# One-core attention, mixture-of-experts and bilinear kernel: head 0 prepared first, similarities turned by transposes, 256- and 512-token chunks mixed in the second stage

## The chip, the cores and the metric

The kernel runs on one core of a Trainium2 chip. The time is device microseconds (us) of one launch; three runs of the kernel before gave 778.71, 779.07 and 779.94 us, median 779.07. Beside them one execution was profiled.

The engines, by the profile's names: PE is TensorE (matrix products; PEld is its load of the stationary operand), DVE is VectorE, ACT is ScalarE, POOL is GpSimd, SP is SyncE, which here only issues transfers. SBUF is the on-chip memory, PSUM the eight banks that PE writes its sums to. Each engine works through its own list of instructions in order.

## The reference

```python
# 1. attention: B=2, H=8, S=768, D=64, 16 centroids a head
q_assign = argmax(einsum('bhsd,hcd->bhsc', q_n, c_n))   # k_assign likewise
mask     = q_assign[:, :, :, None] == k_assign[:, :, None, :]
attn     = softmax(where(mask, scale * q @ k.T, -1e9))
x        = (attn @ v), heads side by side               # 1536 tokens x 512
# 2. mixture of experts: 8 experts, each token to the one with the largest logit
h = relu(x[mask] @ w1[e]);  out[mask] = gate[mask] * (h @ w2[e])   # F = 1024
# 3. bilinear layer: d_ff = 1536
out = ((x @ w_a) * (x @ w_b)) @ w_out
```
Centroids, queries and keys are divided by their norms before the similarity; for a query's or key's own argmax its own norm does not matter, a centroid's does.

## The kernel before

**Attention.** The 16 pairs of (batch, two heads) are 8 steps of `pp`; each has 12 units `s` (two heads, six tiles of 128 queries). A unit is: `scores` (two products of 512 and two of 256 columns, L550 and L551), `rowmax` (a DVE maximum over 768 keys, L559), `expo` (ACT, L564), `etrans` (six 128x128 transposes, L579, copied out by ACT L583 and DVE L585). Once in six units `pv_gen` multiplies by V (L606). The mask is 16 extra rows of K3 and Q3 that `prep_gen` makes for the next `pp` while the units of this one run; it is a generator, and the loop over `s` takes one or two of its steps per unit (`UNITS`, L802). The steps of `prep_gen`: transposes of split rows of K and Q into K2 and Q2 (L425, through three PSUM banks tagged `rot`); copies of K2, Q2 into K3, Q3 by DMA (L429, L430); similarities to the centroids `sm` (L441), copied to `sim`; `st` (L450), which turns six 128x128 tiles of `sim` by a product with `bothr`, a matrix that adds a centroid's rounded and rest part and multiplies by its reciprocal norm; then in `first_gen` (L455) maximum, comparison, index, maximum, comparison on DVE give the one-hot `oh`; `t2` (L495, L518) transposes it into K3 and Q3.

**The start.** For `pp` 0 there is nothing to hide behind: splitting (`split_rows`, L375), both heads' transposes, both heads' `sm` and `st`, then head 0's one-hot, then `scores(0)`. `setup_centroids` (L301) gives its DVE operations one by one between. `keep_warm` (L258) multiplies ones into an unused tile. `load_qk(1)` uses the buffers of `load_qk(0)` (L219, one buffer each).

**Experts.** The weights stream in through four `raw` buffers and are split in two parts. The change does not touch this.

**Bilinear layer.** The five chunks in `CHUNKS` (L33) are 256, 256, 256, 512 and 256 tokens. The list `order` (L1358) goes through the first three together, four columns of `w_a`, `w_b` (128 wide) for a chunk at a time, 36 steps; then the 512-token chunk, 12 steps, and the last one, 12 steps. A step I is `bil1(I)` (24 products, L1119 within `mm3`, then ACT L1311, DVE L1312, ACT L1313, DVE L1317) and `bil2` of an earlier step (L1352; three products of 512 columns per 128 tokens). `bil1` of a 256-token chunk fills half-banks of `et0` or `et1` in turn; of a 512-token chunk two banks, `et0`, `et1` and `pp`, `pv` in turn. Beside that a step narrows one piece of the 64-bit weights (`narrow_a` to `narrow_d`: ACT, three DVE, ACT, DVE), and `load_raw` then asks for a further piece on SP's queue. `X2` and `X2S` (L34, L35) say at which step a chunk's tokens are loaded (`load_x2`) and split on ACT and DVE (`split_x2`).

Of the kernel before, what the change touches and what calls it, by code (L numbers as in the profile page):

```python
# [22 lines left out]
P = 128  # L23
# [12 lines left out]
I0 = 0  # L36
PACE = (1,)
YW = 1
CG0 = 2
# [3 lines left out]
FL1 = 2  # L43
# [4 lines left out]
def kernel(  # L48
# [186 lines left out]
    load_v(0)  # L235
    emb_sb = att.tile([NE, DM], F32, tag="emb", name="emb_sb", bufs=1)
    nc.sync.dma_start(out=emb_sb, in_=expert_emb)
    tau_sb = left.tile([P, 1], F32, name="tau_sb")
    nc.sync.dma_start(out=tau_sb, in_=tau.rearrange("(o n) -> o n", o=1).to_broadcast([P, 1]))
# [8 lines left out]
    both = att.tile([P, 4 * C], F32, name="both", bufs=1)  # L248
# [4 lines left out]
    nc.vector.tensor_reduce(out=mbi, in_=ident5[:, :, 1, :], axis=AX.XY, op=ALU.add)  # L253
    nc.vector.tensor_scalar(out=msc, in0=mbi, scalar1=FAR, scalar2=1.0, op0=ALU.mult, op1=ALU.max)
    nc.vector.tensor_scalar(out=mbi, in0=mbi, scalar1=-FAR, scalar2=None, op0=ALU.mult)
    nc.vector.tensor_add(both.rearrange("p (s c) -> p s c", s=4), ident5[:, :, 0, :], ident5[:, :, 1, :])
# [78 lines left out]
    nc.gpsimd.memset(cbuf.bitcast(F32), 0.0)  # L335
    nc.gpsimd.iota(iota_c, pattern=[[0, 1], [-1, C]], base=C, channel_multiplier=0, allow_small_or_imprecise_dtypes=True)
    identb = att.tile([P, P], BF16, name="identb", bufs=1)
    nc.gpsimd.tensor_copy(identb, ident)

    def setup_rest():  # L340
# [14 lines left out]
        yield  # L355
        nc.vector.reciprocal(rtau, tau_sb)
# [18 lines left out]
    def split_rows(pp):  # L375
# [6 lines left out]
        hss = (slice(0, 1), slice(1, 2)) if pp == 0 else (slice(0, 2),)  # L382
        for hs in hss:
            nc.scalar.copy(c[:, hs, :, :D], kk[:, hs])
            nc.scalar.activation(a[:, hs, :, D:], qq[:, hs], AF.Copy, scale=scale)
        for hs in hss:
            yield
            if pp == 0:
                nc.vector.tensor_sub(c[:, hs, :, D:], kk[:, hs], c[:, hs, :, :D])
                nc.vector.scalar_tensor_tensor(out=a[:, hs, :, :D], in0=qq[:, hs], scalar=scale, in1=a[:, hs, :, D:], op0=ALU.mult, op1=ALU.subtract)  # L390
            else:
                nc.gpsimd.tensor_sub(c[:, :, :, D:], kk, c[:, :, :, :D])
# [5 lines left out]
    def prep_gen(pp):  # L398
# [13 lines left out]
        def evac(dst, src):  # L412
            n[0] += 1
            if n[0] < 7 or n[0] % 2 if pp == 0 else second[0]:
# [5 lines left out]
        for u in range(3):  # L420
            for dst, src in ((K2, c), (Q2, a)):
                pt = bank(F32R, f"t1_{pp}_{u}")
                for j in range(4):
                    h, i = divmod(4 * u + j, NT)
                    nc.tensor.transpose(pt[:, j * P:(j + 1) * P], src[:, h, i, :], identr)  # L425
                evac(dst[:, u * 512:(u + 1) * 512], pt)
                yield

        nc.sync.dma_start(out=K3[:D].bitcast(F32), in_=K2[:D].bitcast(F32))  # L429
        nc.sync.dma_start(out=Q3[:D].bitcast(F32), in_=Q2[D:].bitcast(F32))  # L430

        groups = ((0,), (1,)) if pp == 0 else ((0, 1),)
        sts = []
        for hs in groups:
            slots = [2 * h + isk for h in hs for isk in range(2)]
            sim = att.tile([P, S], F32, tag="sim", name=f"sim_{pp}", bufs=1)
            for lo, w in ((0, 512), (512, 256)):
                pt = bank(F32, f"sm_{pp}_{lo}")
                for sl in slots:
                    h, isk = divmod(sl, 2)  # L440
                    nc.tensor.matmul(pt[:, :w], cbuf[:, 2 * hp + h, 96 - 32 * sl:224 - 32 * sl],  # L441
                                     (Q2, K2)[isk][:, h * S + lo:h * S + lo + w], start=(sl == slots[0]), stop=(sl == slots[-1]))
                evac(sim[:, lo:lo + w], pt[:, :w])
                yield
            yield
            if pp == 0:
                keep_warm(wps[:, :512], FL1)
            st_ = bank(F32, f"st_{pp}")[:, :NT * 64].rearrange("p (t s c) -> p t s c", s=4, c=C)
            for j in range(NT):
                nc.tensor.matmul(st_[:, j], sim[:, j * P:(j + 1) * P], bothr[:, hp, :], start=True, stop=True)  # L450
            n[0] += 1
            sts.append(st_[:, :, slots[0]:slots[-1] + 1, :])
            yield
# [24 lines left out]
        for hs, st_ in zip(groups, sts):  # L478
            ohs = []
            firsts.append((hs, 2 * len(hs), ohs, first_gen(hs, st_, ohs)))  # L480
        for hs, ns, ohs, fg in firsts:
# [5 lines left out]
            if pp == 0:  # L487
                h = hs[0]
                order = [(1, t) for t in range(NT)] + [(0, t) for t in range(NT)]
                for u in range(0, len(order), 4):  # L490
                    if h == 0:
                        keep_warm(wps[:, :512], FL2)
# [17 lines left out]
                    if h == 0:  # L510
                        next(firsts[1][3])
# [16 lines left out]
            if pp == 0 and h == 0:  # L528
                yield
        yield  # L530
# [229 lines left out]
    next(cg)  # L760
    next(cg)
    sg = split_rows(0)
    next(sg)
    next(sg)
    for _ in range(CG0):
        next(cg)
    drain(sg)
    pg = prep_gen(0)
    for i in range(2):
        keep_warm(wps[:, :512], 5)  # L770
        next(pg)
    for i in range(4):
        next(pg)
        for _ in range(3):
            next(cg, None)
    for _ in range(2):
        next(pg)
    drain(cg)
    rest = setup_rest()
    next(rest)  # L780
# [480 lines left out]
    HD = DC // 2  # L1261

    def load_x2(ck):

        at, wd = CHUNKS[ck]
        if ck == 2:
            x = [big.tile([P, DC, CAP], F32R, tag="xe", name=f"x2{n}_{ck}", bufs=2) for n in "hl"]
            x = [[x[m][:, HD * u:HD * u + HD] for u in range(2)] for m in range(2)]
        elif wd == CAP:
            x = new_x(f"b{ck}")  # L1270
            x = [[x[:, m, HD * u:HD * u + HD] for u in range(2)] for m in range(2)]
        else:
            x = [[rawp.tile([P, HD, wd], F32R, tag="raw", name=f"x2_{ck}{m}{u}") for u in range(2)] for m in range(2)]
        for u in range(2):
            nc.sync.dma_start(out=x[1][u].bitcast(F32), in_=ys_v[:, HD * u:HD * u + HD, at:at + wd])
        xT_t["b", ck] = x

    def split_x2(ck, u):

        hi, lo = (x[u] for x in xT_t["b", ck])  # L1280
# [171 lines left out]
```

## Time and profile before

| | us |
|---|---|
| median of three runs | 779.07 |
| the profiled execution | 778.49 |
| its span (first to last instruction) | 776.4 |
| PE busy in the span | 754.8 |
| DVE, ACT, POOL busy | 462.6, 378.4, 106.1 |

The attention fills the span up to about 293 us, the experts up to about 465, the bilinear layer the rest. PE counts as busy from a product's start to a modelled end, and such ends overlap the next start; so what a group of products costs PE is read from the start of one group to the start of the next, not from its duration. The clock that PE was granted stands at 1.00 in all stretches but the last (0.98).

### The profile page before, as it was taken

The numbers are of one execution on the slowest core, as the hardware profiler recorded it, in microseconds if no ns is written. First come the engines' busy times: TensorE is split into PE (matmuls) and PEld (weight loads), VectorE is DVE, ScalarE is ACT, GpSimd is POOL, SyncE is SP. The second block draws the span as 40 slices with busy tenths as digits, with TensorE's granted clock in tenths as the row PEclk, the third lists the DMA queues.
The fourth block names the chain that finished last, engine by engine and source line by source line (L and its number), as shares of the span: only waits on it lengthen the run. The fifth ranks groups of instructions, "written<-read, shape, count | busy, mean of one in ns | idle before, by whom it ended". The sixth has DMA issues, their size and how long they took to land.

```text
span 776.4 us, 13347 instructions
## 1 busy us (share of the span) xinstructions
PE 754.8 (97%) x5097; PEld 648.5 (84%) x5097; DVE 462.6 (60%) x929; ACT 378.4 (49%) x794; POOL 106.1 (14%) x143
## 2 busy tenths in 40 slices
PE   8899999999999988999999999999999999999996
PEld 5667777777777668999999999999999988888995
DVE  6776665787767776378876898877743221121211
ACT  5656766667675665266654555544423211111211
POOL 6203212051300041000000004420001110000201
PEclk9999999999999999999999999999999999999999
DMA  7228133152221026789879866773401000000100
GB/s 187 60 80 270 45 94 87 59 182 96 60 52 32 28 96 225 271 299 296 276 243 275 280 218 186 154 139 113 136 1 55 28 28 1 0 1 1 55 1 27
DMA packets 48519, 91.91 MB, mean 118 GB/s; under 512 B 6328, under 2 KB 21304, under 8 KB 48448
## 3 DMA queue, kind: packets, MB, share of 16 engines
q1 hardware_dynamic: 44240, 81.01, 35.8%
q0 software_dynamic: 2304, 6.31, 2.1%
q10 hardware_dynamic: 1904, 3.67, 1.3%
q8 instruction: 41, 0.67, 0.3%
q14 instruction: 30, 0.25, 0.1%
HBM read 69.27 MB, written 14.04 MB: 107 GB/s over the span
## 4 chain that ended last, share of the span: by engine, by line
PE 32%; issue 22%; DVE 2%; DMA 2%; POOL 1%; ACT 1%; POOLq 0%; DVEq 0%; ACTq 0%
PE ab L1119 11%; PE y L1236 4%; PE o_sc L1352 4%; PE h L1201 3%; PE y L1240 2%; PE h L1119 2%; PE h L1193 2%; DMA raw<-in_moe_w_dram 2%; PE h L1202 1%; DVE w L207 1%; PE y L1241 1%; POOL out_dram L1330 1%; PE o_pp L1352 1%; PE o_pv L1352 1%; PE xT L1100 0%
## 5 line engine op out<-in xcount | busy, mean ns | idle before, releaser
L1312 DVE TENSOR_TENSOR ga<-ab,ga 128x256 f32<-128x256 f32 (+1 forms) x60 | 28.6, 477 | 156.0 <-ACT ga L1311 84.8
L564 ACT ACTIVATE E<-sc,nmx 128x768 f32<-128x768 f32 x96 | 86.8, 904 | 56.3 <-DVE nmx L559 47.3
L1119 PEld LDWEIGHTS ab<-xT_b,w 128*128 128x128 f32 x864 | 107.8, 191 | 2.6
L1119 PE MATMUL ab<-xT_b,w 128*128 128x256 f32 x864 | 109.2, 283 | 0.0
L559 DVE TENSOR_REDUCE nmx<-sc 128x1 f32<-128x768 f32 x96 | 91.4, 953 | 17.1 <-PE sc L551 16.0
L1311 ACT COPY ga<-ab 128x256 f32<-128x256 f32 (+1 forms) x60 | 25.0, 417 | 151.9 <-PE ab L1119 151.9
L579 PEld LDWEIGHTS et<-ident,E 128*128 128x128 f32 x576 | 62.6, 141 | 34.7 <-ACT ET L583 12.5
L1352 PE MATMUL o_sc<-w,g 128*128 128x512 f32 x360 | 90.1, 392 | 0.0
L579 PE MATMUL et<-ident,E 128*128 128x128 f32 x576 | 82.2, 279 | 4.8 <-ACT E L564 2.8
L585 DVE COPY ET<-et 128x384 f32<-128x384 f32 x96 | 52.6, 548 | 54.9 <-PE et L579 54.8
L1352 PEld LDWEIGHTS o_sc<-w,g 128*128 128x128 f32 x360 | 65.4, 189 | 12.1
L606 PE MATMUL pv<-ET,v 128*64 128x384 f32 (+2 forms) x408 | 73.0, 479 | 0.6 <-ACT ET L583 0.5
L550 PE MATMUL sc<-K,Q 80*128 80x512 f32 x192 | 72.8, 380 | 0.5 <-DMA Q<-Q 0.5
L207 DVE TENSOR_TENSOR w<-raw,w 128x1024 fp32r<-128x1024 f32 x48 | 58.2, 1219 | 17.2 <-ACT w L206 16.6
L1119 PE MATMUL ab<-x,w 128*128 128x512 f32 x288 | 67.7, 391 | 0.2 <-DVE ot L1329 0.2
L1119 PEld LDWEIGHTS ab<-x,w 128*128 128x128 f32 x288 | 54.0, 188 | 12.1 <-DVE ot L1329 0.6
L551 PE MATMUL sc<-K,Q 128*128 128x512 f32 x192 | 61.7, 342 | 0.0
L1236 PE MATMUL y<-hh,w 128*128 128x256 f32 (+3 forms) x416 | 59.4, 290 | 0.8 <-issue 0.8
L206 ACT CAST w<-raw 128x1024 fp32r<-128x1024 f32 x48 | 50.3, 1051 | 16.1 <-DMA raw<-in_moe_w_dram 11.1
L1313 ACT CAST g<-ga 128x256 fp32r<-128x256 f32 (+1 forms) x60 | 26.9, 449 | 59.7 <-DVE ga L1312 59.7
L1236 PEld LDWEIGHTS y<-hh,w 128*128 128x128 f32 x416 | 54.5, 190 | 1.2 <-issue 0.9
L583 ACT COPY ET<-et 128x384 f32<-128x384 f32 x96 | 45.7, 476 | 2.7 <-PE et L579 2.6
(272 smaller groups left out, 1253.9 us busy)
## 6 DMA issues: line engine op xcount, KB each, us to landing
raw<-in_moe_w_dram SPq DMA_DIRECT2D x48, 512.0 KB, 5.1
w<-in_moe_w_dram SPq DMA_DIRECT2D x16, 512.0 KB, 6.6
raw<-in_moe_w_a_dram SPq DMA_DIRECT2D x12, 512.0 KB, 4.5
raw<-in_moe_w_b_dram SPq DMA_DIRECT2D x12, 512.0 KB, 4.8
raw<-in_moe_w_out_dram SPq DMA_DIRECT2D x12, 512.0 KB, 5.2
xs_d<-zero SPq DMA_DIRECT2D x8, 512.0 KB, 6.2
xe<-xs_d ACTq DMA_DIRECT2D x7, 512.0 KB, 7.2
v<-in_v_dram SPq DMA_DIRECT2D x8, 384.0 KB, 3.1
```

What stands on the lines that cost most here:

```text
L206: nc.scalar.copy(hi, w)
L207: nc.vector.tensor_sub(lo, w, hi)
L550: nc.tensor.matmul(ps[:, lo:hi], Q3[:, qs], K3[:, h * S + lo:h * S + hi], start=True, stop=False)
L551: nc.tensor.matmul(ps[:, lo:hi], Q2[:, qs], K2[:, h * S + lo:h * S + hi], start=False, stop=True)
L559: nc.vector.tensor_reduce(out=nmx[pp][:, h, t:t + 1], in_=sc[s], axis=AX.X, op=ALU.max, negate=True)
L564: nc.scalar.activation(e, sc.pop(s), AF.Exp, bias=nmx[pp][:, h, t:t + 1], accum_out=sums[pp][:, t, h:h + 1])
L579: nc.tensor.transpose(pt[:, j * P:(j + 1) * P], e[:, kt * P:(kt + 1) * P], ident)
L585: nc.vector.tensor_copy(dst, src)
L606: nc.tensor.matmul(pv[h * D:(h + 1) * D, :], vt[:, h, kt, :], ets[g, h][:, kt, :n * P], start=(kt == 0), stop=(kt == NT - 1))
L1119: nc.tensor.matmul(ps, s_, m_, start=(i == 0), stop=(i == len(ops) - 1))
L1236: nc.tensor.matmul(ys_ps[e][j // 2][:, j % 2, :wd], w[:, m_, ff, j * P:(j + 1) * P], s_, start=(f == 0 and i == 0 and j % 2 == 0), stop=(l ...
L1352: nc.tensor.matmul(o_ps[ck][t], s_[:, t * P:(t + 1) * P], w_[:, m_], start=(f == 0 and i == 0), stop=(J == I and f == NF2 - 1 and i == 2))
```

## The change

In attention, for `pp` 0: head 0's rows are split, transposed and copied first, and its similarities are computed with the tokens as the stationary operand (`near_c`: twelve products of 32 columns, each 128 tokens by 16 rounded and 16 rest parts), so that no turning is needed; DVE adds the two parts (`sv`). Head 1's transposes come next; its `near_c` and one-hot come after `scores(1)`. The centroids are normalized before they are rounded (the product with `bothr` goes). For `pp` 1 to 7 `near_all` is `sm` as before, but `turn_all` turns `sim` by plain transposes in two groups of three, and DVE adds the parts of each group. The loads for `pp` 0 get buffers of their own (those of `E`), so those of `pp` 1 wait for nothing; `load_v(0)` and two small loads are issued later.

In the bilinear layer the chunks are 256, 512, 512 and 256 tokens: the first two go together (24 steps), then the others. A 512-token step narrows two pieces. `bil2` lags one step behind in 512-token steps. The halves of a chunk are loaded one by one.

In the diff, L31 on:

```diff
-CHUNKS = ((0, 256), (256, 256), (512, 256), (768, 512), (1280, 256))
-X2 = {-7: 0, 0: 1, 4: 2, 27: 3, 39: 4}
-X2S = {-3: [(0, 0), (0, 1)], 2: [(1, 0), (1, 1)], 6: [(2, 0), (2, 1)], 29: [(3, 0)], 31: [(3, 1)], 42: [(4, 0)], 43: [(4, 1)]}
+CHUNKS = ((0, 256), (256, 512), (768, 512), (1280, 256))
+X2 = {-7: [(0, 0), (0, 1)], 0: [(1, 0)], 2: [(1, 1)], 19: [(2, 0), (2, 1)], 27: [(3, 0), (3, 1)]}
+X2S = {-3: [(0, 0), (0, 1)], 2: [(1, 0)], 3: [(1, 1)], 20: [(2, 0)], 21: [(2, 1)], 30: [(3, 0)], 31: [(3, 1)]}
...
-            qk_raw[n, pp] = att.tile([P, 2, NT, D], F32, tag=n, name=f"{n}_{pp}", bufs=1)
+            qk_raw[n, pp] = att.tile([P, 2, NT, D], F32, tag=n if pp else "E", name=f"{n}_{pp}", bufs=1 if pp else 2)
...
+        def near_c(hs, t0, t1, sv):
             slots = [2 * h + isk for h in hs for isk in range(2)]
+            ns = len(slots)
+            w = 2 * C
+            pt = bank(F32, f"sm_{pp}_{t0}")
+            for t in range(t0, t1):
+                for i, sl in enumerate(slots):
                     h, isk = divmod(sl, 2)
+                    o = ((t - t0) * ns + i) * w
+                    nc.tensor.matmul(pt[:, o:o + w], (Q2, K2)[isk][:, h * S + t * P:h * S + (t + 1) * P], cbuf[:, 2 * hp + h, own], start=True, stop=True)
+            nc.vector.tensor_reduce(out=sv[:, t0:t1].rearrange("p t s c -> p (t s) c"),
+                                    in_=pt[:, :(t1 - t0) * ns * w].rearrange("p (a z c) -> p a c z", z=2, c=C), axis=AX.X, op=ALU.add)
...
+        def turn_all(sim, sv, t0, t1):
+            pt = bank(F32, f"st_{pp}_{t0}")
+            for t in range(t0, t1):
+                nc.tensor.transpose(pt[:, (t - t0) * P:(t - t0 + 1) * P], sim[:, t * P:(t + 1) * P], ident)
+            nc.vector.tensor_reduce(out=sv[:, t0:t1].rearrange("p t s c -> p (t s) c"),
+                                    in_=pt[:, :(t1 - t0) * P].rearrange("p (a z c) -> p a c z", z=2, c=C), axis=AX.X, op=ALU.add)
...
+        if pp == 0:
+            for h in range(2):
+                for dst, src in ((K2, c), (Q2, a)):
+                    for g0 in (h * NT, h * NT + HALF):
+                        turned(dst, src, g0, g0 + HALF)
+                        if h:
+                            next(firsts[0][3], None)
+                        yield
+                dup(slice(h * S, (h + 1) * S))
+                if h == 0:
+                    first_of(h)
+                    yield
...
-            pab = [ps_t.tile([P, wd], F32, tag=t, name=f"ab{z}_{I}") for z, t in enumerate((("et0", "et1"), ("pp", "pv"))[I % 2])]
+            pab = [ps_t.tile([P, wd], F32, tag=f"et{z}", name=f"ab{z}_{I}") for z in range(2)]
...
-    order = [(ck, 4 * c + ff) for c in range(NF2 // 4) for ck in range(3) for ff in range(4)]
-    order += [(ck, f) for ck in (3, 4) for f in range(NF2)]
+    order = [(ck, 4 * c + ff) for c in range(NF2 // 4) for ck in range(2) for ff in range(4)]
+    order += [(ck, f) for ck in (2, 3) for f in range(NF2)]
```

How the lists of the engines move, at three places. First DVE's list from the first row maximum (`nmx` of `sc_0`) on; before:

```order
L559 TENSOR_REDUCE nmx_0_358<-sc_0_352 128x1
L559 TENSOR_REDUCE nmx_0_358<-sc_1_362 128x1
L471 TENSOR_TENSOR oh_0_368<-smm_0_329,mx_0_330 128x192
L585 COPY ET_0_0_0_374<-et_0_1_380 128x3x128
L506 TENSOR_SCALAR K3_0_178<-t2_0_0_385 16x512
L559 TENSOR_REDUCE nmx_0_358<-sc_2_398 128x1
```

and now:

```order
L593 TENSOR_REDUCE nmx_0_331<-sc_0_325 128x1
L593 TENSOR_REDUCE nmx_0_331<-sc_1_335 128x1
L432 TENSOR_REDUCE sv_0_341<-sm_0_0_342 128x192
L462 TENSOR_REDUCE mx_0_357<-sv_0_341 128x12
L619 COPY ET_0_0_0_363<-et_0_1_369 128x3x128
L464 TENSOR_TENSOR smm_0_356<-sv_0_341,mx_0_357 128x192
L466 TENSOR_TENSOR smm_0_356<-smm_0_356,iota_c_106 128x192
L470 TENSOR_REDUCE mx_0_357<-smm_0_356 128x12
L593 TENSOR_REDUCE nmx_0_331<-sc_2_377 128x1
L473 TENSOR_TENSOR oh_0_383<-smm_0_356,mx_0_357 128x192
```

Head 1's sum, maximum, comparison, index and maximum stand behind the first two row maxima now; before, all but the last comparison stood ahead of them.

Second, PE's list where `pp` 2 is turned, during unit 15 (`et` are the unit's transposes, `sc_17` the scores two units on); before:

```order
L579 MATMUL et_15_0_904<-ident_96,E_15_872 128x128 x3
L579 MATMUL et_15_1_909<-ident_96,E_15_872 128x128 x3
L450 MATMUL st_2_914<-bothr_113,sim_2_860 128x64 x6
L550 MATMUL sc_17_921<-K3_1_425,Q3_1_424 128x512
L551 MATMUL sc_17_921<-K2_1_423,Q2_1_422 128x512
```

and now:

```order
L613 MATMUL et_15_0_906<-ident_92,E_15_874 128x128 x3
L613 MATMUL et_15_1_911<-ident_92,E_15_874 128x128 x3
L446 MATMUL st_2_0_916<-ident_92,sim_2_862 128x128 x3
L446 MATMUL st_2_3_921<-ident_92,sim_2_862 128x128 x3
L584 MATMUL sc_17_926<-K3_1_425,Q3_1_424 128x512
```

The place is the same; the turning takes two `rot` banks instead of one, so its second group takes the third bank after `et_15_0`, that is the same bank.

Third, SP's list at the start of the bilinear layer (`raw_64` to `raw_68` are pieces of weights, `xT_b1`, `x2l_2` and `x2_111` tokens read from `ys_d`, `ys_7` the last expert's result); before:

```order
L152 DMA raw_64_7062<-in_moe2_w_b_dram 128x1024
L1275 DMA xT_b1_7077<-ys_d_75 128x2x256 x2
L152 DMA raw_65_7111<-in_moe2_w_b_dram 128x1024
L152 DMA raw_66_7160<-in_moe2_w_b_dram 128x1024
L1256 TENSOR_LOAD ov_i_3500
L1256 ISA x2
L1257 REGISTER_ALU
L1257 DMA ys_d_75<-ys_7_7130 128x4x176
L152 DMA raw_67_7225<-in_moe2_w_b_dram 128x1024
L152 DMA raw_68_7274<-in_moe2_w_out_dram 128x1024
L1275 DMA x2l_2_7290<-ys_d_75 128x2x256 x2
```

and now:

```order
L151 DMA raw_64_7087<-in_moe2_w_b_dram 128x1024
L1316 DMA xT_b1_7102<-ys_d_75 128x2x512
L151 DMA raw_65_7135<-in_moe2_w_b_dram 128x1024
L151 DMA raw_66_7184<-in_moe2_w_b_dram 128x1024
L1316 DMA x2_111_7200<-ys_d_75 128x2x512
L1294 TENSOR_LOAD ov_i_3525
L1294 ISA x2
L1295 REGISTER_ALU
L1295 DMA ys_d_75<-ys_7_7154 128x4x176
L151 DMA raw_67_7250<-in_moe2_w_b_dram 128x1024
```

The second half of chunk 1 is asked for behind `raw_66`; it is split in step 3 and first used in step 4.

## Rows read from the trace of the kernel before

**Rows 1.** Busy time by stretch: us, PE, PEld, DVE, ACT, POOL (instructions), clock, DMA.
```profile
20.00:40.00 20.00, 16.58 (x120) 13.34 (x118) 14.88 (x27) 11.86 (x26) 5.65 (x3) 1.00 0.21 50
40.00:60.00 20.00, 18.39 (x131) 13.61 (x131) 16.04 (x41) 13.20 (x28) 0.47 (x2) 1.00 0.31 104
...
100.00:200.00 100.00, 99.41 (x697) 74.97 (x696) 71.35 (x138) 70.19 (x156) 26.89 (x24) 1.00 0.36 102
...
465.00:520.00 55.00, 55.00 (x397) 52.17 (x396) 43.80 (x86) 27.03 (x58) 21.96 (x23) 1.00 0.74 160
```

**Rows 2.** Timeline of the first 19 us: start, us, engine, instruction [idle before].
```profile
2.90 0.70 PE L311 MATMUL pc<-ident,cent_sb 128*64 128x128 f32 x4 [2.90 <-DMA cent_sb<-in_centroids_dram]
...
3.53 2.31 PE L261 MATMUL wps<-ones 128*128 128x512 bf16 x5
...
5.27 0.64 DVE L390 SCALAR_TENSOR_TENSOR qr<-q,qr 128x384 fp32r<-128x384 f32 x1
...
7.41 0.15 DVE L275 RECIPROCAL c_r<-c_g 128x1 f32<-128x1 f32 x1
...
9.35 0.17 DVE L283 RECIPROCAL c_r<-c_g 128x1 f32<-128x1 f32 x1
...
10.86 0.60 PE L261 MATMUL wps<-ones 128*128 128x512 bf16 x2
10.96 0.58 SPq L430 DMA_DIRECT2D Q<-Q  x1
...
14.22 0.35 DVE L460 TENSOR_REDUCE mx<-st 128x12 f32<-128x192 f32 x1
...
15.84 0.36 DVE L471 TENSOR_TENSOR oh<-smm,mx 128x192 bf16<-128x192 f32 x1
...
18.06 0.37 SPq L223 DMA_DIRECT2D q<-in_q_dram  x1
...
18.95 0.47 PE L550 MATMUL sc<-K,Q 80*128 80x512 f32 x1 [0.51 <-DMA Q<-Q]
```

**Rows 3.** Timeline of one pair's turning, in the middle of the attention.
```profile
133.43 0.48 ACT L583 COPY ET<-et 128x384 f32<-128x384 f32 x1 [0.34 <-PE et L579]
...
133.56 1.45 PE L450 MATMUL st<-bothr,sim 128*128 128x64 f32 x12
...
134.81 0.48 PE L550 MATMUL sc<-K,Q 80*128 80x512 f32 x1
...
135.61 0.82 PE L579 MATMUL et<-ident,E 128*128 128x128 f32 x6
...
136.19 0.48 PE L550 MATMUL sc<-K,Q 80*128 80x512 f32 x1
...
136.69 0.55 DVE L460 TENSOR_REDUCE mx<-st 128x24 f32<-128x384 f32 x1
```

**Rows 4.** Waits from 60 to 280 us: total, times, longest.
```profile
ACT E L564 <- DVE nmx L559: 40.6, 37, 3.0
```

**Rows 5.** Timeline of PE in the bilinear layer, 256- and 512-token steps.
```profile
481.44 3.04 PE L1119 MATMUL ab<-xT_b,w 128*128 128x256 f32 x24
...
485.70 3.04 PE L1119 MATMUL ab<-xT_b,w 128*128 128x256 f32 x24
...
699.98 5.60 PE L1119 MATMUL ab<-x,w 128*128 128x512 f32 x24
...
708.14 5.60 PE L1119 MATMUL ab<-x,w 128*128 128x512 f32 x24
```

**Rows 6.** Bilinear layer: SP's timeline, landing of `raw` and of tokens, ACT's split.
```profile
474.61 4.46 SPq L152 DMA_DIRECT2D raw<-in_moe_w_b_dram  x2
...
DMA to landing us min/median/max: 3.4/4.9/8.3
...
x<-ys_d SPq DMA_DIRECT2D x2, 512.0 KB, 3.7
...
600.45 1.05 ACT L1281 CAST x<-x 128x1024 fp32r<-128x1024 f32 x1
```

More of the change, by code (lines that the diff above doesn't have):

```diff
@@ L42 @@
 FL4 = 30
-FL1 = 2
+FL1 = 6
 FL2 = 2
@@ L419, in prep_gen @@
         eng = nc.vector if pp < 2 else nc.gpsimd
[L420 to L429, printed above, removed]
@@ new lines, in near_all @@
+        def near_all(sim, lo, w):
+            pt = bank(F32, f"sm_{pp}_{lo}")
+            for sl in range(4):
+                h, isk = divmod(sl, 2)
+                nc.tensor.matmul(pt[:, :w], cbuf[:, 2 * hp + h, (3 - sl) * 2 * C:(7 - sl) * 2 * C],
+                                 (Q2, K2)[isk][:, h * S + lo:h * S + lo + w], start=(sl == 0), stop=(sl == 3))
+            evac(sim[:, lo:lo + w], pt[:, :w])
+        def turn_all(sim, sv, t0, t1):
[4 more added lines that the diff above has]
+                                    in_=pt[:, :(t1 - t0) * P].rearrange("p (a z c) -> p a c z", z=2, c=C), axis=AX.X, op=ALU.add)
@@ L477, in prep_gen, with first_of @@
         firsts = []
-        for hs, st_ in zip(groups, sts):
+        def first_of(h):
+            sv = new_sv((h,))
+            near_c((h,), 0, NT, sv)
             ohs = []
-            firsts.append((hs, 2 * len(hs), ohs, first_gen(hs, st_, ohs)))
+            firsts.append(((h,), 2, ohs, first_gen((h,), sv, ohs)))
+        if pp == 0:
[3 more added lines that the diff above has]
+                        turned(dst, src, g0, g0 + HALF)
+                        if h:
+                            next(firsts[0][3], None)
+                        yield
+                dup(slice(h * S, (h + 1) * S))
+                if h == 0:
+                    first_of(h)
+                    yield
+        else:
+            for g0 in range(0, 2 * NT, 4):
+                for dst, src in ((K2, c), (Q2, a)):
+                    turned(dst, src, g0, g0 + 4)
+                    yield
+            dup(slice(0, 2 * S))
+            sv = new_sv((0, 1))
+            sim = att.tile([P, S], F32, tag="sim", name=f"sim_{pp}", bufs=1)
+            for lo, w in ((0, 512), (512, 256)):
+                near_all(sim, lo, w)
+                yield
+            turn_all(sim, sv, 0, HALF)
+            yield
+            turn_all(sim, sv, HALF, NT)
+            yield
+            ohs = []
+            firsts.append(((0, 1), 4, ohs, first_gen((0, 1), sv, ohs)))
         for hs, ns, ohs, fg in firsts:
@@ L759 @@
     cg = setup_centroids()
-    next(cg)
-    next(cg)
     sg = split_rows(0)
-    next(sg)
-    next(sg)
+    rest = setup_rest()
+    next(rest)
     for _ in range(CG0):
         next(cg)
+    keep_warm(wps[:, :512], 9)
+    next(sg)
+    for _ in range(CG1):
+        next(cg)
+    next(sg)
+    pg = prep_gen(0)
+    for _ in range(4):
+        next(pg)
+        for _ in range(2):
+            next(cg, None)
+    keep_warm(wps[:, :512], 1)
+    next(sg)
+    drain(cg)
+    keep_warm(wps[:, :512], 1)
     drain(sg)
-    pg = prep_gen(0)
-    for i in range(2):
-        keep_warm(wps[:, :512], 5)
+    next(pg)
+    load_small()
+    load_v(0)
+    for _ in range(4):
         next(pg)
[L772 to L780, printed above, removed]
     drain(split_rows(1))
@@ L1261, with load_x2 @@
     HD = DC // 2
-    def load_x2(ck):
+    x2_t = {}
+    def load_x2(ck, u):
         at, wd = CHUNKS[ck]
[L1266 to L1271, printed above, removed]
-        else:
[L1273 to L1276, printed above, removed]
+        if wd == CAP:
+            if u == 0:
+                x2_t[ck] = new_x(f"b{ck}")
+            x = [x2_t[ck][:, m, HD * u:HD * u + HD] for m in range(2)]
+        elif ck == 1 and u == 0:
+            x = new_x("b1").rearrange("p m j n -> p m (j n)").rearrange("p m (j n) -> p m j n", n=wd)
+            x = [x[:, m] for m in range(2)]
+        elif ck == 1:
+            x = [big.tile([P, HD, wd], F32R, tag="xe", name=f"x2_{ck}{m}{u}", bufs=2) for m in range(2)]
+        else:
+            x = [rawp.tile([P, HD, wd], F32R, tag="raw", name=f"x2_{ck}{m}{u}") for m in range(2)]
+        nc.sync.dma_start(out=x[1].bitcast(F32), in_=ys_v[:, HD * u:HD * u + HD, at:at + wd])
+        xT_t["b", ck, u] = x
     def split_x2(ck, u):
-        hi, lo = (x[u] for x in xT_t["b", ck])
+        hi, lo = xT_t["b", ck, u]
         nc.scalar.copy(hi, lo.bitcast(F32))
@@ L1293, in bil1 @@
         at, wd = CHUNKS[ck]
-        xh, xl = xT_t["b", ck]
+        x = [xT_t["b", ck, u] for u in range(2)]
         if wd == CAP:
@@ L1399 @@
             next(pg_, None)
-        if I in X2:
-            load_x2(X2[I])
+        for ck, u in X2.get(I, ()):
+            load_x2(ck, u)
         for ck, u in X2S.get(I, ()):
```

122 lines of the change are left out of this document (54 added, 68 removed).

## The prediction
> **What bounds the kernel now.** I read the busy times by stretch first [rows 1]. From 100 to 200 us PE is busy for 99.41 of 100, and from 465 to 520 us for all 55: there PE is the bound, and a microsecond of its work that goes is a microsecond of time. From 20 to 60 us it has gaps, 3.42 and 1.61 us, together 5.03, while DVE has 5.12 and 3.96: there chains through ACT and DVE set the time, and PE's work alone doesn't. Ahead of that stands the start, up to the first score at 18.95 us [rows 2], in which nothing of the real work runs. Then I read the timelines of the three places which the change touches [rows 2, 3, 5], and last the waits and the transfers that could take the gain back [rows 4, 6]. The experts between keep their own list, so I let that stage shift as a whole.
>
> **The change part by part.** The sum is made against the profiled execution, 778.49 us, of which the span is 776.4 and 2.1 lie outside it; the median of the runs is 0.58 above it.
>
> *1. The first score.* Now: head 0's query rests are ready on DVE at 5.27 + 0.64 = 5.91 us, as before. Behind them eight one-column operations of the centroids' norm and the scaling: from the reciprocal at 7.41 to the one at 9.35 are ten such, 0.19 each [rows 2], so 1.75 and 7.7 us. The centroid transpose took 0.70 (8.4); rounding on ACT and the rest on DVE, neither above the 0.35 of a 192-column operation, bring it to 9.2 at most. Twelve products of `near_c` with a weight load each cost about what the twelve records of `st` cost, 134.81 - 133.56 = 1.25 [rows 3]: 10.5. The sum of the two parts reads 384 values like the maximum of 0.55 [rows 3]: 11.1. The five operations to the one-hot ran from 14.22 to 16.20, 1.98 [rows 2]: 13.1. From there to the first score it was 18.95 - 16.20 = 2.75, and 0.51 of that was a wait for the copy of Q, issued at 10.96 behind the loads of `pp` 1. Now the copies are half as large and ahead of everything but those loads, which start some 3 us earlier; so 2.25 to 2.75, and the first score at 15.4 to 15.8: a lead of 3.35 us. The keep-warm products before it (24 now, 20 before) cost nothing: they stand where PE waits for DVE, and two of them took 0.60 at 10.86. Five took 2.31 at 3.53, so PE's products ran at half pace then, though the clock column shows 1.00 throughout; now nine start without waiting for the centroids, at about 1.2 us, so that PE is not slower than before when real work comes.
>
> How much of the lead lasts? Behind the first row maxima DVE now also has head 1's sum (0.55), four of the five operations to the one-hot (1.6) and the three small mask operations (0.65 by their kin): 2.8 us that used to fill DVE's idle start. PE has head 1's twelve products (1.25) there as well. If DVE's gaps hide all, and pair 1's cheaper turning counts, the part gives -3.9; if nothing is hidden, 3.35 is paid back with 2.8 and 1.25, +0.7. DVE has 9.1 us of gaps in that stretch, over three times what it gets, so I take a value nearer the first end: -2.4. Head 1's copies of K2 and Q2 also come later: SP issues them behind the load of `q` for `pp` 2, which waits until POOL has done with `q` (18.06 before [rows 2], about 1 us later now as ACT's casts are later). Issued by 20.5 they are there at about 24, just when head 1's first score has its one-hot; the wait is in the range, not in the sum.
>
> *2. Turning, pairs 2 to 7.* `st` costs PE 1.25 us (133.56 to 134.81). Six transposes of the same form cost 136.19 - 135.61 = 0.58 [rows 3]. That would save 0.65. But the second group of three takes the bank of the unit's first transposes, which ACT copies out until 133.43 + 0.48 = 133.91; with the hand-over it starts near 134.0 and the score behind it at 134.35, a saving of 0.46. I take 0.53: six pairs, -3.2 (ends -2.8 and -3.9). DVE's two added sums a pair, 2 x 0.55, lie beside PE's work: DVE is busy for 71 of 100 us [rows 1], a pair lasts some 33.
>
> Here a rule speaks against the change. The rows show transposes 0.10 us apart [rows 3]. The Trainium skill (TensorE: Matmul & The Clock Gate, Part 4: PE-mode transpose) gives about 275 ns for one within a kernel; by that six are 1.65 us, each pair loses 0.4, the part is +2.4 and the time 777.5. The 576 transposes of the units are the same instruction, so I go by the rows.
>
> *3. The mixed chunks.* A 256-token step takes 485.70 - 481.44 = 4.26 us, a 512-token step 708.14 - 699.98 = 8.16 [rows 5]: a product of 512 columns costs less than two of 256. Twelve times two short steps become twelve long ones: 12 x (8.52 - 8.16) = -4.3. The long steps now have one pair of banks instead of two; DVE must have multiplied a step's halves before PE comes to the second bank again, two thirds of a step later (5.4 us), and needs 0.7. Two narrowings in a long step are the same rate, 3 in 12.4 us of PE, and DVE's load (43.80 of 55, [rows 1]) stays.
>
> *4. A new wait in step 4.* The second half of chunk 1 is issued behind `raw_66`. The two `raw` issues at 474.61 end at 479.07 [rows 6], so it goes out at 479.1; the first half, at 471, is early enough. Step 4 starts at 481.44 [rows 5] and needs it after four products of 8.16 / 36 = 0.227, at 482.35. It lands after 4.9 us, the median of a `raw` of the same 512 KB: 484.0; ACT's split takes 1.05: 485.05. PE waits 2.7 us. With 3.7 us (tokens, later, with little other traffic) it is 1.5, with 8.3 (the longest `raw`) 6.1. Behind it in PE's list stands everything; nothing hides it, and since PE is the bound it isn't caught up. ACT waits with it, but has slack.
>
> The rows here are 3.7 to 8.3 us for 512 KB. The Trainium skill (DMA: Bandwidth & Descriptors, Anatomy of one DMA) fits 2.0 us plus the bytes at 436 GB/s; an estimate by that page is 3.2 us, a wait of 1.0 and a time of 770.2.
>
> Chunk 2 is loaded when the narrowing is over and lies four steps ahead; chunk 3 as before. They cost nothing.
>
> *Sum:* -2.4 - 3.2 - 4.3 + 2.7 = -7.2; 771.3 for the profiled execution, 771.9 for the median: **772**. Ends: -3.9 - 3.9 - 4.3 + 1.5 = -10.6, so 768.5; and +0.7 - 2.8 - 4.3 + 6.1 = -0.3, so 778.8.
>
> **Rivals.**
> - *Everything is hidden*: the start's lead lasts, the load lands early. For it: DVE's gaps from 20 to 60 us [rows 1], and tokens that landed in 3.7 us [rows 6]. Against: `raw_66` flows right ahead of this load. 768.5.
> - *The start gives its lead back*: head 1's chain is late on DVE, or its copies hold the first score of head 1; part 1 is about 0, the time 774.4. For it: DVE's list in that place; against: before, head 1's first score waited too.
> - *The turning gives nothing*, because two groups of three that wait for banks pay their full latency each (0.82 for six shows 0.24 beyond the 0.58): part 2 about 0, 775.1.
> - *Slower: DVE sets the pace in the attention.* Then PE's savings are void and each DVE operation is paid: 6 x 1.10 = +6.6 in pairs 2 to 7, +2.8 - 3.35 at the start, -4.3 + 2.7 in the bilinear layer: +4.45, 783.5. For it: ACT's exponentials wait 40.6 us for row maxima [rows 4]. Against: PE has 0.59 us of gaps in 100, so those waits end before PE runs dry. It decides once DVE has no gap of 1.1 us left in a pair, and it has some 9.
>
> **How the numbers follow.** Chances: my forecast 0.52; everything hidden 0.20; the lead given back 0.13; the turning without gain 0.06; slower 0.05; 0.04 for two of these together, about no change. 8 in 10 lie from 767 to 777, which holds the ends but the last 2 us of the upper one, and adds 1.5 below for pauses of the experts' stage that I can't price. Around 0.2%, 1.6 us, is what a measurement here tells from none: faster by more 0.91, within 0.04, slower 0.05.
>
> **What would show it.** Part 1: the first score near 15.6 us, and the first score of unit 12 about 2 us earlier than before. Part 2: in a pair's turning 0.6 to 0.8 us between the first transpose of `sim` and the next score. Part 3: 8.16 us a long step also in the first 24 steps. Part 4: a PE gap of 1.5 to 6 us ahead of the fifth product of step 4, ended by ACT's split. I am wrong if PE shows gaps in the attention that end on row maxima, if the long steps last over 8.3 us, or if the experts' stage changes its length by over 1 us.

## The result and the profile after

The changed kernel took 783.31 us (median of nine runs, 782.37 to 789.10; the kernel before in the same runs 779.10): a ratio of 1.0063, 95% interval 1.0045 to 1.0081. It is slower, by 0.6%, and the time lies outside the range. The profiled execution took 782.37 us (span 780.2), 3.88 more than that of before. By the starts of the same products in both traces (us; units and scores are numbered from 0, so unit 12 is the first of pair 1):

| | before | after | difference | forecast |
|---|---|---|---|---|
| first score | 18.95 | 16.40 | -2.55 | -3.35 |
| score of unit 12 | 51.98 | 51.79 | -0.19 | -2.4 |
| from there to the last score | 227.35 | 224.10 | -3.25 | -3.2 |
| last score to first expert product | 14.64 | 15.09 | +0.45 | 0 |
| experts | 170.70 | 170.64 | -0.06 | 0 |
| bilinear layer, first to last product | 305.12 | 312.15 | +7.03 | -1.6 |

The forecast held in the middle of the attention and failed at the start (2.2 us) and in the bilinear layer (8.6 us). First stretches of the changed kernel, three of them those of [rows 1], the last three around step 4; the column behind POOL is the granted clock:

```profile
10.00:20.00 10.00, 9.63 (x60) 5.96 (x60) 6.31 (x13) 5.36 (x11) 6.62 (x4) 0.83 0.42 128
20.00:30.00 10.00, 7.67 (x54) 6.58 (x53) 7.15 (x17) 5.05 (x13) 0.00 (x0) 0.83 0.27 79
...
20.00:40.00 20.00, 16.41 (x113) 13.88 (x112) 16.79 (x36) 11.95 (x27) 5.76 (x3) 0.91 0.39 100
40.00:60.00 20.00, 17.90 (x128) 13.21 (x128) 15.42 (x38) 12.19 (x26) 0.62 (x1) 1.00 0.24 82
100.00:200.00 100.00, 99.21 (x691) 74.23 (x689) 76.29 (x148) 69.97 (x154) 26.86 (x24) 1.00 0.35 100
...
479.00:483.00 4.00, 0.47 (x3) 0.04 (x1) 1.78 (x4) 0.06 (x1) 1.58 (x2) 1.00 0.51 184
483.00:493.00 10.00, 5.04 (x12) 3.98 (x13) 1.22 (x1) 2.22 (x3) 0.00 (x0) 0.50 0.30 89
493.00:496.00 3.00, 3.00 (x14) 2.41 (x13) 0.62 (x2) 0.00 (x0) 0.00 (x0) 0.96 0.00 0
```

In [rows 1] the clock is 1.00 everywhere. Here it is at its lower level, 0.50 or 1.2 GHz, from 483 to 493, while and after PE stood still, and it was there for parts of 10 to 30 us. Next the chain of waits in step 4 (start, us, what):

```profile
476.06 6.62 DMA x<-ys_d
...
482.84 3.92 DMA ys_d<-ys
...
486.87 1.05 ACT x L1322
...
487.96 7.30 PE ab L1157 x20
```

The load of the half chunk, which the forecast had in this place, is followed by a transfer that it didn't have there: the put, that is the transfer that writes expert 7's rows (`ys_7`) into the tensor `ys_d`. The waits on SP's queue (total, times, longest) say why it comes so late, and those of ACT who waits for it:

```profile
SPq L1295 <- DMA x<-ys_d: 5.5, 1, 5.5
```
```profile
ACT x L1322 <- DMA ys_d<-ys: 7.8, 1, 7.8
```

The put writes the tensor that the load reads, at a row known only at run time, and waits for the load to land. ACT's split then waits for the put. PE's timeline shows the price:

```profile
487.96 2.07 PE L1157 MATMUL ab<-x,w 128*128 128x512 f32 x4 [8.50 <-ACT x L1322]
...
495.11 0.84 PE L1394 MATMUL o_pp<-w,g 128*128 128x512 f32 x3
...
497.83 1.07 PE L1157 MATMUL ab<-xT_b,w 128*128 128x512 f32 x4
...
505.99 1.07 PE L1157 MATMUL ab<-xT_b,w 128*128 128x512 f32 x4
```

PE is idle for 8.50 us; its next 20 products take 495.11 - 487.96 = 7.15 us instead of 20 x 0.227 = 4.54, which is 2.6 for the clock. With the 4.3 that the long steps give: 8.50 + 2.6 - 4.3 = 6.8 of the 7.03. The last two rows are one long step apart: 505.99 - 497.83 = 8.16, as in [rows 5].

The start, beside [rows 2], and where the first head-1 score (25.05) and the first of pair 1 (51.79) stand:

```profile
8.65 0.28 PE L431 MATMUL sm<-cbuf,Q 128*128 128x32 f32 x1
...
11.43 2.25 PE L261 MATMUL wps<-ones 128*128 128x512 bf16 x6
...
12.42 0.36 DVE L473 TENSOR_TENSOR oh<-smm,mx 128x192 bf16<-128x192 f32 x1
...
13.61 0.59 PE L530 MATMUL t<-identb,oh 128*16 128x128 bf16 x4
...
16.40 0.50 PE L584 MATMUL sc<-K,Q 80*128 80x512 f32 x1
...
18.87 0.37 SPq L222 DMA_DIRECT2D q<-in_q_dram  x1
...
19.81 0.59 SPq L452 DMA_DIRECT2D Q<-Q  x1
...
25.05 0.50 PE L584 MATMUL sc<-K,Q 80*128 80x512 f32 x1 [0.27 <-ACT Q L409]
...
51.79 0.48 PE L584 MATMUL sc<-K,Q 80*128 80x512 f32 x1 [1.06 <-DMA Q<-ohT]
```

The one-hot begins at 12.42, 3.42 earlier than the 15.84 of [rows 2], and ends at 12.78, a little ahead of the 13.1 of the forecast. Six keep-warm products beside it take 2.25 us where two took 0.60 before, and the first product that reads the one-hot starts behind them at 13.61, 0.8 us after the one-hot is there. Unit 12 waits 1.06 us for its mask rows; in the kernel before it waited for nothing:

```profile
51.98 0.47 PE L550 MATMUL sc<-K,Q 80*128 80x512 f32 x1
```

And one pair's turning, beside [rows 3]:

```profile
131.44 0.87 PE L613 MATMUL et<-ident,E 128*128 128x128 f32 x6
132.15 0.95 PE L446 MATMUL st<-ident,sim 128*128 128x128 f32 x6
132.86 0.48 PE L584 MATMUL sc<-K,Q 80*128 80x512 f32 x1
```

132.86 - 132.15 = 0.71 us for six transposes, against 1.25 for `st`.

### The profile page after: what moved, and what is told of

The parts are those of the page before. It is cut to its first block, busy times and chain, and to the rows that moved or that the text cites. A ratio compares the mean times of both kernels' runs of the same rounds, so it can differ in the third digit from the quotient of the medians.

```text
span 780.2 us, 12634 instructions
## 1 busy us (share of the span) xinstructions
PE 750.3 (96%) x4761; PEld 630.9 (81%) x4761; DVE 465.2 (60%) x910; ACT 374.2 (48%) x769; POOL 106.2 (14%) x145
## 4 chain that ended last, share of the span: by engine, by line
issue 28%; PE 24%; DMA 4%; DVE 2%; POOL 1%; ACT 1%; POOLq 0%; SPq 0%; ACTq 0%; DVEq 0%
PE ab L1157 6%; PE y L1274 4%; PE h L1239 3%; PE y L1278 2%; DMA raw<-in_moe_w_dram 2%; PE h L1157 2%; PE h L1231 2%; PE o_sc L1394 1%; PE h L1240 1%; PE y L1279 1%; POOL out_dram L1372 1%; DMA x<-ys_d 1%; DVE w L206 1%; ACT w L205 1%; DMA ys_d<-ys 1%
## 5 line engine op out<-in xcount | busy, mean ns | idle before, releaser
L1353 DVE TENSOR_TENSOR ga<-ab,ga 128x256 f32<-128x256 f32 (+1 forms) x48 | 26.8, 558 | 160.6 <-PE ab L1157 114.3
L1157 PE MATMUL ab<-x,w 128*128 128x512 f32 x432 | 109.6, 394 | 8.5 <-ACT x L1322 8.5
L1157 PE MATMUL ab<-xT_b,w 128*128 128x256 f32 (+1 forms) x720 | 114.4, 306 | 0.0
L1157 PEld LDWEIGHTS ab<-xT_b,w 128*128 128x128 f32 x720 | 99.4, 192 | 7.6
L1157 PEld LDWEIGHTS ab<-x,w 128*128 128x128 f32 x432 | 81.9, 190 | 26.4 <-ACT x L1322 8.9
L1352 ACT COPY ga<-ab 128x256 f32<-128x256 f32 (+1 forms) x48 | 23.0, 480 | 129.8 <-PE ab L1157 126.6
L1394 PE MATMUL o_sc<-w,g 128*128 128x512 f32 x288 | 69.5, 390 | 0.0
L1354 ACT CAST g<-ga 128x256 fp32r<-128x256 f32 (+1 forms) x48 | 24.7, 514 | 84.1 <-DVE ga L1353 84.1
L1394 PEld LDWEIGHTS o_sc<-w,g 128*128 128x128 f32 x288 | 53.9, 188 | 11.3
```

Of the source, the lines that this page charges most:

```text
L1157: nc.tensor.matmul(ps, s_, m_, start=(i == 0), stop=(i == len(ops) - 1))
L1394: nc.tensor.matmul(o_ps[ck][t], s_[:, t * P:(t + 1) * P], w_[:, m_], start=(f == 0 and i == 0), stop=(J == I and f == NF2 - 1 and i == 2))
```

## The experiments

All are timed against the kernel before; where nothing else is said, they are edits of the changed kernel. "Gap" is PE's idle time in step 4, ahead of the first product that reads the half chunk. Gaps, starts and clocks come from the one profiled execution of each kernel, times from the median of 4 to 12 runs; single runs lie up to 4.9 us from the median of their kernel.

**The two halves of the change.** Each keeps one half and takes the other from the kernel before.

```diff
 # attention_only
-CHUNKS = ((0, 256), (256, 512), (768, 512), (1280, 256))
+CHUNKS = ((0, 256), (256, 256), (512, 256), (768, 512), (1280, 256))
...
 # bilinear_only, against the kernel before
-CHUNKS = ((0, 256), (256, 256), (512, 256), (768, 512), (1280, 256))
+CHUNKS = ((0, 256), (256, 512), (768, 512), (1280, 256))
...
```

> The attention's half of the change alone, with the bilinear layer as before. If the lead of 3.0 us that the changed kernel's trace shows at the attention's end comes through the experts: 779.1 - 3.0 = 776.1. If the experts or the bilinear layer's loads swallow it: 779.1.

> The bilinear layer's half of the change alone, with the attention as before. If the loss lies in step 4's gap and the clock behind it (8.5 + 2.65 against 4.3 won by the long steps): 779.1 + 6.9 = 786. If it needs the attention's half too (a late or early arrival in the bilinear layer): 779.1 - 1.6 = 777.5, as predicted for this half.

attention_only: 776.71 us, ratio 0.9963 (0.9948 to 0.9977), as expected: the attention's lead comes through the experts. bilinear_only: 787.44, 1.0095 (1.0078 to 1.0113), somewhat over the 786 expected; its gap is 9.5 us:

```profile
PE ab L1117 <- ACT x L1282: 9.5, 1, 9.5
```

So the loss is the bilinear half's own, and the attention's half wins 0.4% by itself.

**Load and put at other places.**

```diff
 # put_first
-            ready.append((G + YW, e, yts))
+            ready.append((G + (YW if e < NE - 1 else 0), e, yts))
 # load_early
-X2 = {... 0: [(1, 0)], 2: [(1, 1)], ...}
+X2 = {... 0: [(1, 0), (1, 1)], ...}
 # put_and_load_early: both
```

> Two theories for the 8.50 us that PE waits in step 4. Theory 1, a chain: the load of the half chunk is issued at 476.06 and lands 6.6 us later; the put of expert 7's rows, which writes the same tensor, waits for that landing and goes out at 482.84; the tile that ACT's split writes lies in the buffer which that put reads, so the split waits for the put as well. Here the put stands ahead of the load: it should go out near 471.6, the split then waits for the load alone (476.1 + 6.6 + 1.1 for the split), the gap is 483.8 - 479.5 = 4.3 us, and the time 783.3 - 4.2 = 779.1, or 776.4 if the clock then doesn't fall. Theory 2, the one of the prediction: the load alone is late, the put has no part in it. The load is no earlier here, so the gap stays 8.5 us and the time 783.3.

> The half chunk is asked for in step 0 instead of step 2, the put stays where it is. Theory 1 (chain): the load has landed by 475, the put follows raw_66 at about 476.1 and lands 4 us later, the split is done at 481.2: a gap of 1.7 us, too short for the clock to fall; 783.3 - 6.8 - 2.65 = 773.9. Theory 2 (the load alone): no gap, 783.3 - 8.5 - 2.65 = 772.1.

> The put a step earlier and the load in step 0. Both theories: no gap in step 4. If the clock at half from 483.0 to 493.2 follows from the gap, it stays at 1.00 here and the time is 783.3 - 8.5 - 2.65 = 772.1. If the clock falls for another reason (the wide steps themselves), it falls here as well: 774.8.

The times were 784.04 (1.0048, 1.0028 to 1.0068), 780.85 (1.0016, 1.0004 to 1.0029) and 779.92 (1.0009, 0.9989 to 1.0030); the gaps 7.43, 6.91 and 5.71 us. put_first's time is near theory 2's, the others near neither's; no gap is as expected. (The profiled executions lie 2.3 us below the median in put_first and 2.6 and 2.1 above it in the others.) The releasers, though, are those of the chain. put_first, waits of SP's queue and ACT's timeline:

```profile
SPq L1316 <- DMA ys_d<-ys: 4.2, 1, 4.2
```
```profile
486.99 1.04 ACT L1322 CAST x<-x 128x1024 fp32r<-128x1024 f32 x1 [6.74 <-DMA x<-ys_d]
```

Now the load waits for the put, which went out at 475.12 instead of the 471.6 expected and landed 6.3 us after its issue. load_early, the chain and ACT's timeline:

```profile
471.54 7.97 DMA x<-ys_d
...
479.67 7.79 DMA ys_d<-ys
```
```profile
487.56 1.04 ACT L1322 CAST x<-x 128x1024 fp32r<-128x1024 f32 x1 [5.75 <-DMA ys_d<-ys]
```

The load, issued at 471.54, had landed at 479.51, before the put went out at 479.67; PE ran dry only at 481.74, and the split still waited for the put. So the load alone is not what is late, and the prediction's own theory falls here. With both early (ACT at 486.44, released by a put issued at 479.19) the order is the same. What failed in the expectations is, for put_first, that a put ahead ties the load just as the load tied the put, and for the others the durations: I had 4 us for a put and 6.6 for a load, and here a put took 6.3 to 7.8 us and the early load 7.5 to 8; the transfer engines are 0.69 busy from 461 to 479 us in the changed kernel.

**The put out of the chain.** Expert 7's rows go to two buffers of another ring (the buffers of one tag, used in turn), so that the split shares none with them.

```diff
 # ys_apart; ys_apart_load_early has load_early's X2 too
+            if e == NE - 1:
+                yts = [big.tile([P, 2, CAP], F32, tag="hh", name=f"ys_{e}{u}", bufs=4) for u in range(2)]
...
             yts = big.tile([P, DC, CAP], F32, tag="xe", name=f"ys_{e}", bufs=2)
```

> Expert 7's rows lie in two buffers of the ring hh and not in the one that ACT's split of the half chunk writes; the load stays in step 2. In the three kernels before, the gap of step 4 stayed 5.7 to 7.4 us although the load or the put went out earlier, since the two are chained either way and each took 5.5 to 7.9 us to land. Theory 1 (the chain of load, put and shared buffer): without the shared buffer the split waits for the load alone, 476.1 + 6.6 + 1.1; a gap of 4.3 us and 783.3 - 4.2 = 779.1, or 776.4 if the clock stays. Rival (transfers in these microseconds are slow whatever waits for what): the gap stays over 6 us, 781 or more.

> As the one before, and the load in step 0. Theory 1: no gap in step 4, the clock stays at 1.00 there, 783.3 - 8.5 - 2.65 = 772.2. Rival: the load issued at about 469 lands as late as 479 (7.5 us, as it did when the put was early), the split is at 480 and PE waits under 1 us: 773; or the two hh buffers are missed by steps 4 and 5 (the put lands at 487), 774.

ys_apart: 780.36 (1.0004, 0.9988 to 1.0020), gap 5.13. The split now waits for the load alone (what ACT's idle time ended on, at the tile `x`; then the clock):

```profile
  DMA x<-ys_d: 3.9, 1
```
```profile
484.00:491.00 7.00, 5.14 (x12) 4.12 (x13) 1.23 (x1) 2.21 (x3) 0.00 (x0) 0.52 0.33 101
```

The load was issued at 477.33 and took 7.4 us: 0.8 over the expectation, as is the gap. The time lies between the 779.1 of theory 1 and the 781 of the rival; the rival's gap (over 6 us) is wrong, and the releaser is the one that theory 1 names. ys_apart_load_early: 774.55 (0.9935, 0.9916 to 0.9955), where theory 1 had 772.2 and the rival 773 or 774. Its ACT, and the window that was at 0.50:

```profile
477.63 0.41 ACT L1364 CAST g<-ga 128x256 fp32r<-128x256 f32 x1 [1.00 <-PE o_pv L1404]
...
478.46 1.04 ACT L1332 CAST x<-x 128x1024 fp32r<-128x1024 f32 x1
```
```profile
483.00:493.00 10.00, 10.00 (x46) 8.28 (x45) 5.58 (x10) 2.89 (x5) 1.76 (x2) 1.00 0.37 64
```

The split waits for no transfer any more, and the clock stays at 1.00: its fall in step 4 goes with the gap, as the expectation of put_and_load_early had asked. 1.1 us of gap are left, and the rows say from where: the split stands behind the rounding of step 3, which waited 1.00 us, and that rounding writes to the ring that expert 7's rows now use, so the rival's second half has a part in it. The profiled execution is the fastest of the six (771.56); what the others lose no trace shows.

**The start.**

```diff
 # start_warm
     load_v(0)
+    keep_warm(wps[:, :512], 3)
...
+                    elif u < 8:      # head 1's one-hot; wps2 is a bank of the tag pv
...
+                        keep_warm(wps2, 1 if u else 6)
 # start_warm_copy: that, and
-    load_qk(2)
     while (0, 0) not in prep_n:
         next(pg)
+    load_qk(2)
```

> The changed kernel with ten more keep-warm products at the start: three behind head 0's near_c, seven ahead of head 1's transposes of the one-hot, where PE waits. Theory A, the clock takes the start's lead: no fall of the clock from 10 to 30 us, first score at 15.1 instead of 16.4, sc_4 at 28.6 instead of 29.6, and sc_3 held at 25.06 by the copies of head 1; 783.3 - 1.0 = 782.3. Theory B, the lists of DVE and ACT take it: the clock may stay, sc_12 is at 51.8 as now, 783.3.

> As start_warm, and head 1's copies of K2 and Q2 are issued ahead of the loads of pp 2 that wait for POOL (at about 12.5 instead of 19.3). Theory A with the copies: sc_3 at 23.7 instead of 25.05, sc_4 at 27.2, sc_12 at 49.0 to 50.5 if pair 1's one-hot follows, 783.3 - 2.8 = 780.5. Theory B: sc_3 is earlier, but sc_12 stays near 51.8, since pair 1's mask rows are late on DVE, ACT and SP; 783.3 - 0.3 = 783.0.

start_warm in its windows and PE's timeline:

```profile
10.00:20.00 10.00, 9.75 (x71) 6.87 (x71) 7.27 (x14) 5.97 (x13) 6.17 (x4) 1.00 0.42 121
20.00:30.00 10.00, 8.27 (x63) 5.80 (x61) 7.42 (x18) 4.49 (x11) 0.44 (x1) 1.00 0.28 79
```
```profile
25.06 0.48 PE L588 MATMUL sc<-K,Q 80*128 80x512 f32 x1 [1.11 <-DMA Q<-Q]
```

The clock stays; the first score is at 15.57, unit 4's at 28.55 (after: 29.55), unit 12's at 50.80, the last at 274.82 instead of 275.89. In the trace this is theory A, and head 1's copies hold the score at 25.06. The time shows none of it: 784.39 (1.0058, 1.0037 to 1.0080). In the profiled execution the experts took 172.7 us instead of 170.6, with more waits for split weights, and the gap of step 4 was 9.0. start_warm_copy, PE's timeline:

```profile
24.31 0.50 PE L588 MATMUL sc<-K,Q 80*128 80x512 f32 x1 [0.27 <-ACT Q L409]
...
50.09 0.47 PE L588 MATMUL sc<-K,Q 80*128 80x512 f32 x1 [1.05 <-DMA Q<-ohT]
```

The copies no longer hold head 1's score, unit 12 starts 1.7 us earlier than in the changed kernel, within the 49.0 to 50.5 of theory A, and the last score is at 274.17. The time, 782.64 (1.0034, 1.0018 to 1.0050), is nearer to the 783.0 of theory B than to the 780.5 of theory A; by the two ratios it is 2.3 us below the changed kernel, though the intervals overlap. One place where the lead goes stands in the trace: from the last score to the first expert product it takes 16.81 us instead of 15.09, with the clock at 0.91 from 276 to 294 us where the changed kernel had 1.00.

**The turning undone.** An edit of attention_only.

```diff
-            turn_all(sim, sv, 0, HALF)
...
+            for t in range(NT):
+                nc.tensor.matmul(st[:, t], sim[:, t * P:(t + 1) * P], both, start=True, stop=True)
             yield
-            turn_all(sim, sv, HALF, NT)
...
```

> attention_only with one part undone: pairs 1 to 7 are turned by twelve weight loads' worth of one product with a 0/1 matrix (six products of 64 columns, each in two passes) instead of six transposes and two sums on DVE. If the turning gives 0.5 us a pair, as the distance of the score starts in the two traces says: 776.7 + 3.2 = 779.9, and no lead over the kernel before is left at the attention's end beyond what the start keeps. If the lead comes from elsewhere: 776.7.

779.44 (0.9999, 0.9988 to 1.0010), 779.9 expected: the 0.37% (2.9 us) of attention_only is gone. PE's timeline of one pair:

```profile
135.06 1.45 PE L516 MATMUL st<-both,sim 128*128 128x64 f32 x12
136.32 0.48 PE L589 MATMUL sc<-K,Q 80*128 80x512 f32 x1
```

136.32 - 135.06 = 1.26 us, as [rows 3].

**All together.** all_mended is ys_apart_load_early with start_warm_copy and the load at step -1; split_earlier moves the split besides.

```diff
-X2 = {... 0: [(1, 0)], 2: [(1, 1)], ...}
+X2 = {... -1: [(1, 1)], 0: [(1, 0)], ...}
 # split_earlier
-X2S = {... 2: [(1, 0)], 3: [(1, 1)], ...}
+X2S = {... 2: [(1, 0), (1, 1)], ...}
```

> The changed kernel with expert 7's rows in buffers of their own, the half chunk's load ahead of the first bilinear step, the ten keep-warm products and head 1's copies ahead of the loads of pp 2. If the start's gain adds to that of the bilinear layer: 774.55 less 0.3% (2.3 us) = 772.2, and 771.2 if the last 1.1 us of step 4's gap go with the still earlier load. If the experts' stage takes the start's gain back in its waits for transfers: 774.5.

> all_mended with the half chunk split in step 2 instead of step 3. If the 1.1 us that PE still waits in step 4 is the place of the split in ACT's list (it stood behind the rounding of step 3, which itself waited 1.0 us for a buffer): no gap, 773.1 - 1.1 = 772.0. If the load or the put still sets it: the gap stays 1.1 us, 773.1.

all_mended: 773.09 (0.9907, 0.9892 to 0.9923); the gap stayed 1.1 us, so the still earlier load did nothing for it. The time lies between the 772.2 and the 774.5 expected, so how much of the start's gain adds is open; in its profile, too, the stretch to the first expert product took 16.86 us at a clock of 0.91. split_earlier: 770.32 (0.9883, 0.9858 to 0.9907), below the 772.0 expected. Its PE in the stretch of step 4:

```profile
475.00:500.00 25.00, 25.00 (x117) 20.89 (x116) 17.65 (x30) 10.59 (x19) 5.91 (x7) 1.00 0.52 123
```

Busy for all 25 us: the gap was the place of the split in ACT's list. Its time is 1.9 us better than all_mended's by the two ratios, whose intervals overlap. This kernel is faster than both the kernel before and the changed one, with all parts of the change in it.

## Why the prediction was wrong, step by step

*Step 4 is the one that failed.* It said: the load "lands after 4.9 us", "ACT's split takes 1.05: 485.05. PE waits 2.7 us", at most 6.1. It followed the load and its one reader and left out what else that reader needs: the split writes a second tile, from the same ring of two buffers (tag `xe`) as `ys_7`, so `ys_7` must have left; and its put must wait for the load, since both touch `ys_d`. The order of SP's list before the prediction showed the put right behind the load, and I priced neither wait. The runs show the chain: with the buffer apart the releaser changes from the put to the load (ys_apart), and with the load early as well the wait for transfers goes (ys_apart_load_early). The measured gap is 8.50 us, with 2.6 more for the clock behind it, against 2.7 in the sum. The load itself took 6.6 us, not 4.9, which alone would have been a gap of 4.3, within the stated 1.5 to 6.1; the other 4.2 are the put. The Trainium skill (DMA: Bandwidth & Descriptors, Anatomy of one DMA) has 2.0 us plus the bytes at 436 GB/s, for a transfer that GpSimd's software path issues; the estimate of 3.2 us for 512 KB that the prediction made from it, for a transfer of SP, is half of the measured 6.6, which decides.

*The clock is missing from the sum altogether.* It stood at 1.00 in all stretches of before but the last, and I took that for a property of the kernel. In all eight profiled kernels whose gap in step 4 was 5.1 to 9.5 us it went to 0.50 within the gap and was still there for some of the work behind it; in the three with gaps of 1.1 and 0 us it stayed at 1.00. In the changed kernel that cost the 2.6 us.

*Step 1: the mechanism half right, the size wrong.* The first score came 2.55 us earlier instead of 3.35, and 0.19 of it lasted to unit 12 instead of 2.4. The forecast set head 1's extra work against DVE's gaps and let the keep-warm products cost nothing. The rows show the clock instead: at 0.83 on average from 10 to 20 and again from 20 to 30 us in the changed kernel, 1.00 in start_warm. At the lower clock the keep-warm products, which the one-hot should have hidden, held up the next product by 0.8 us; in load_early, with the clock at 1.00 there, it starts 0.05 us after the one-hot. The same list of the attention, run in load_early, kept the clock to the first score and had it at 15.07, below the 15.4 to 15.8 forecast. It lost the clock behind that (0.50 from 25 to 30 us) and had unit 12 at 52.44, later than the changed kernel: a lead at the first score alone is worth little.

Keeping PE fed gives 1.0 us at unit 12 (50.80 against 51.79), taking head 1's copies out from behind `q` another 0.7. That wait was named in step 1 and left out of the sum; it is hidden in the changed kernel only because the one-hot is as late. The last 0.5 of the forecast 2.4 goes between unit 4 and unit 12, which takes 22.24 us in the changed kernel and 22.26 in start_warm_copy against 21.78 before, although pair 1's turning is already cheaper: it is the wait of 1.05 to 1.07 us for the mask rows at unit 12. Pair 1's one-hot is not late (44.85 us, before 45.20), but ACT copies it only at 47.59 (46.87); why, no run tests.

*Step 2 was right:* 3.25 us from unit 12 on against 3.2, and 0.71 a turning in the middle of the 0.6 to 0.8. The rule that spoke against it (the Trainium skill, TensorE: Matmul & The Clock Gate, Part 4: PE-mode transpose) gives about 275 ns for one transpose within a kernel. The trace agrees with that as the length of one: the record of a transpose of `st` lasts 273 ns in the median. But they overlap, six of them take PE 0.71 us from start to start, 0.12 each, so six times 275 ns was the wrong use of that figure.

*Step 3 was right:* 8.16 us a long step in the first 24, and the bilinear layer takes 302.37 us in all_mended, with 1.1 of gap left, and 300.88 in split_earlier, with none, against 305.12 before: -4.2, beside -4.3 in the sum.

*The rival "slower"* named DVE in the attention as its place. PE is busy for 99.21 of 100 us there, as before; it was slower for another reason, and that its 783.5 lies 0.2 from the measured 783.31 is luck. So is the end: the kernel with its waits mended comes to 770.32, 1.6 below the 771.9 of the sum. But the sum had counted 2.7 us of wait in step 4, and this kernel has none, and its start is not the one that was forecast; that agreement does not make the forecast right. (One rival is 0.1 off in its own sum: with part 1 at 0 the time is 774.3, not 774.4.)

## What to carry to other kernels

Before a moved load is priced, list for its first reader every buffer that it reads and writes, who held each before, and every transfer on the same tensor whose rows are only known at run time: the load is late when the last of these is, and taking one link away helps little while another is tied to it. Where PE is the bound, price a gap like those here (5.1 to 9.5 us) at its length, and the work behind it at the lower clock. And a lead at the start is worth what the next queue lets through: look at what each copy stands behind.

## What the runs showed of the hardware

The clock also fell where PE had hardly stood still. In the changed kernel PE is busy for 4.43 of the 5 us from 5 to 10 and for 1.81 of the 2 from 10 to 12, with twelve 32-column products from 8.65 on and twelve transposes from 10.01 on, and the clock is at 0.50 from 12 to 15; in the four kernels with three more 512-column products ahead of those transposes it stays at 1.00 there. Nor does the same list always lose it there: in load_early and ys_apart it didn't, and the first score of load_early is 1.33 us earlier than the changed kernel's. Second, the put took 3.9 us from issue to landing in the changed kernel and 6.3 to 7.8 where it went out earlier, the half chunk's load 6.6 and 7.5 to 8: what is asked for earlier here lands later after its issue. It stands there among the weights' transfers, which I read from the queue's busy share and did not test apart.
